# Late weight splits behind the last scatters, later row reads, and a shorter one-hot step in a three-stage kernel

## The chip, the cores and the metric

The program runs on 1 core of one Trainium2 chip. Its time is the device time in microseconds of one execution. The kernel before takes 622.37 us as the median of 3 runs (622.19 to 624.54). The one execution that the profiler took lasted 627.96 us, with a span of 626.2 us from its first to its last instruction.

## The reference

Three layers follow each other. The first is an attention with a state that is updated token by token. The second sends each of the 1536 tokens (2 sequences of 768) to one of 8 experts. The third adds a Fourier transform over tokens and features to each token, normalises, and applies a two-layer perceptron.

```python
def _moe_ref(x, w_gate, w_local, w1, w2):
    ...
            fresh_e = int(np.argmax(logits[b, s]))
            if s == 0 or local_gate[b, s] < 0.5:
                e = fresh_e
            else:
                e = prev_e if prev_e >= 0 else fresh_e
            ...
            h = np.maximum(x[b, s] @ w1[e], 0.0)
            out[b, s] = p[e] * (h @ w2[e])

def _moe2_ref(x, w_ch1, w_ch2):
    X = np.fft.fft(x, axis=1)
    X = np.fft.fft(X, axis=2)
    mixed = np.real(X).astype(np.float32)
    u = x + mixed
    mu = np.mean(u, axis=-1, keepdims=True)
    var = np.mean((u - mu) ** 2, axis=-1, keepdims=True)
    un = (u - mu) / np.sqrt(var + 1e-06)
    ch = np.maximum(un @ w_ch1, 0.0) @ w_ch2
    return (u + ch).astype(np.float32)
```

## The kernel before

Products are made in three passes of split numbers: every fp32 operand becomes a high part (ScalarE, a copy to fp32r) and a low part (VectorE, the original minus the high part), and high*high, low*high and high*low are summed in PSUM.

**Routing** (`route`, L735). From the gate's logits VectorE finds each token's expert (`Ot`, a one-hot row of 8 per token), TensorE counts ranks inside the expert (`rk`, L781 and L783), and VectorE turns the rank into a half (`hi`) and a slot (`rm`). `oh` is the one-hot of the slot; `Wr` carries the token's number in the column of its expert. Thirteen products (`st`, L803) then give a table of token numbers by slot, from which GpSimd gathers rows. `parts` (L811) makes `ph`, number times half, and then `Wr`.

**Experts** (`moe_main`, L940). 32 steps `q`, four for each expert. `whi(q)` (ScalarE, L888) and `wlo(q)` (VectorE, L891) split the step's weights; `wlo(q)` then asks for the weights of step q+6 on the SP queue. `xtr` transposes gathered rows and splits them (L904 to L907), `h` makes the first layer (L916 to L919), `o` the second (L927). At an expert's last step two tiles of results are scaled (`ot`, L932), and `scatter` (L936) writes the rows to their places in `x2d` in DRAM by an indirect DMA that GpSimd issues. `dec` decodes the third layer's weights from a packed form along the way. Behind the last step stand `WARMM` products that fill TensorE's time, `wlo(35)`, and the splits of steps 36 and 37, which are weights of the third layer. The order is that of the code.

**Third layer** (`mixer`, L1375). Each sequence `b` comes back as three blocks of two tiles, `xa` (L1088), in the order 1, 2, 0. Sums and differences of blocks (`sums`, `difs`: tiles `d` and `e`) are split (`zh`, `zl`), multiplied with tables along tokens (`yp`, L1195), evacuated (`Y`) and multiplied along features (`fp`, L1206). Half of the result, `q`, is copied out, `m` combines the halves (L1218, L1219), and `m` is added to `ur`, which holds the sequence's rows in another order: four of six tiles by one SP transfer (L1094), two mirrored ones by indirect DMA (L1098). Then come statistics (`bs`, `ag`, `vs`), the normalised rows `un`, their transpose `up`, its split `uT`, and the perceptron: `mp` (L1330) with `mh` and `ml`, and `mop` (L1356). A further `WARM` products on the first block (L1312) fill TensorE's time before the first `yp`.

The order of this third stage is not that of the code. `Order` (L44) runs generators against assumed costs and emits an engine's next instruction by priority; `eng` (L1103) lets an addition go to VectorE or GpSimd, whichever the plan takes to be done first. So an added wait or another `WARM` moves many instructions.

Of the kernel before, what the change touches and what calls it, by code (L numbers as in the profile page):

```python
# [729 lines left out]
class Rest:  # L730
# [4 lines left out]
    def route(s,keep,pool,ps,lg):  # L735
# [40 lines left out]
        V.tensor_copy(out=e,in_=ei)  # L776
        Ot=s.Ot=pool.tile([128,12,8],F16,name="Ot")
        V.tensor_tensor(out=Ot,in0=it,in1=b3(e),op=ALU.is_equal)

        rk=P("rk",[128,13,8])  # L780
        nc.tensor.matmul(out=rk[:,0:12],lhsT=K["upper"][:,0:128],rhs=Ot,start=True,stop=True,skip_group_check=True)  # L781
        for j in range(12):
            nc.tensor.matmul(out=rk[:,j+1:13],lhsT=ones,rhs=Ot[:,j:j+1].to_broadcast([128,12-j,8]),start=False,stop=True,skip_group_check=True)  # L783
        rank=s.rank=pool.tile([128,12],F32,name="rank")
# [5 lines left out]
        s.Wr=T("W",[128,4,2,12,8],F16); s.ph=T("ph",[128,4,2,12],F16); pp=s.pp=pool.tile([128,4,12],F16,name="pp")  # L790
# [8 lines left out]
        V.tensor_copy(out=pp[:,0],in_=tok)  # L799
        s.parts(0)  # L800
# [139 lines left out]
    def moe_main(s):  # L940
        dec=s.decoding(); s.sc=[]; s.scattered=[]; last=None
        s.chosen()
        s.wlo(0); s.wlo(1)
        for k in range(3): s.xtr(0,k,"h",3)
        s.wlo(2)
        next(dec)
        for q in range(32):
            e,g=divmod(q,4)
            if g==0 and e<7: s.gather(e+1)
            x=s.h(q)  # L950
            if g and e<7: s.xtr(e+1,g-1)
            s.whi(q+4)
            if last: s.o(q-1,last)
            last=x
            s.wlo(q+3)
            if q==1: s.parts(1)
            if q==2: s.parts(2); s.parts(3)
            if q==3: s.slots_p()
            if g==1:
                while s.sc: s.scatter()  # L960
            if q==26: s.tables(0)
            if q==29: s.tables(1)
            if q>2:
                for _ in range(1+(g==0)): next(dec,None)
        for t in range(2):
            s.o(31,last,(t,))
            while s.sc: s.scatter()
        p=s.ps.tile([128,2,256],F32,tag="h",name="wp",bufs=3)
        for _ in range(s.WARMM): s.nc.tensor.matmul(out=p[:,0,0:128],lhsT=s.K["ident"],rhs=s.K["ident"],start=True,stop=True)
        s.wlo(35)  # L970
        for _ in dec: pass
        for q in (36,37):
            s.whi(q); s.wlo(q)

    WARMM=24
# [102 lines left out]
    def load(s,b):  # L1078

        nc,o=s.nc,s.o  # L1080
        yield ("+","xa")
        xa=s.xa[b]={}
        v=s.x2d[768*b:768*b+768].rearrange("(a p) d -> p a d",p=128)
        for n,i in enumerate((1,2,0)):
            yield ("Q",475)
            if n!=1: T=s.rawp.tile([128,1552],F32,tag="raw",name="xa",bufs=6)
            t=T[:,768*(n%2):768*(n%2)+768].rearrange("p (a d) -> p a d",d=384)
            nc.sync.dma_start(out=t,in_=v[:,i:6:3])  # L1088
            xa[i],xa[i+3]=t[:,0],t[:,1]
            o.add(s.arrive(f"xa{b}{i}",1850+1100*n*(1-b)+900))  # L1090
        ur=s.ur[b]=s.fp.tile([128,6,384],F32,tag=f"ur{b}",name="ur",bufs=1)
        w=s.x2d[768*b:768*b+768].rearrange("(p a) d -> p a d",a=6)
        yield ("Q",475)
        nc.sync.dma_start(out=ur[:,0:4],in_=w[:,0:4])  # L1094
        yield f"xa{b}0"
        for k in (4,5):
            yield ("P",1040)
            nc.gpsimd.indirect_dma_start(out=ur[:,k],out_offset=None,in_=s.x2d,in_offset=bass.IndirectOffsetOnAxis(ap=s.K["mirror"][:,2*b+k-4:2*b+k-3],axis=0))  # L1098
        o.add(s.arrive(f"ur{b}",4000))
# [79 lines left out]
    WARM,PHASE=18,0  # L1179
# [303 lines left out]
```

## Time and profile before

| | |
|---|---|
| median of 3 runs | 622.37 us |
| the profiled execution's own time | 627.96 us |
| its span | 626.2 us |
| PE busy | 507.9 us (81%) |
| DVE busy | 421.7 us (67%) |
| ACT busy | 323.7 us (52%) |
| POOL busy | 88.1 us (14%) |
| chain that ended last | PE 38%, issue 13%, POOL 3%, DVE 2% |

The attention takes the span to about 250 us, routing to 267 us, the experts to 410 us and the third layer the rest. The busy shares are means over stages that differ: what counts for an edit is who waits for whom where the edit stands. PE is TensorE, DVE VectorE, ACT ScalarE, POOL GpSimd, SP the engine that issues most transfers.

### The profile page before, as it was taken

The page shows a single profiled execution, that of the slowest core. Times are in us where ns is not written, and L with a number is a line of the kernel's source. Part 1 is how long each engine was busy: PE and PEld are TensorE (multiplying, and loading weights), DVE is VectorE, ACT ScalarE, POOL GpSimd, SP SyncE. Part 2 cuts the span into 40 slices and gives each one's busy share as a digit, 9 for nine tenths or more (in the row PEclk, how much of TensorE's full clock was granted, in tenths as well). Part 3 has the DMA queues.
Part 4 walks back from the last instruction along what each step waited for, and adds up shares of the span by engine and source line. Part 5 has one row for each costly group of instructions (what it writes and reads, how often), then busy time and mean ns, then how long its engine had stood idle before and what let it go on. Part 6 is the DMA issues. An engine that isn't in the chain of part 4 may idle for free.

```text
span 626.2 us, 12592 instructions
## 1 busy us (share of the span) xinstructions
PE 507.9 (81%) x4986; PEld 482.3 (77%) x4986; DVE 421.7 (67%) x950; ACT 323.7 (52%) x745; POOL 88.1 (14%) x89
## 2 busy tenths in 40 slices
PE   0333047894888999599999999978899999999997
PEld 0233037784778898589999999977799998998997
DVE  7968997868997963687788788767886731221122
ACT  3465177877788897346665656543454321111111
POOL 5000000000000000223212232243640000000010
PEclk9955558877989999599999999989699999999999
DMA  6722230341331525699789795235000000010010
GB/s 231 143 59 77 67 62 8 113 93 51 77 70 28 95 49 165 197 312 349 263 286 326 274 304 187 93 133 188 1 1 1 14 13 1 2 50 1 1 50 26
DMA packets 71438, 69.85 MB, mean 112 GB/s; under 512 B 44286, under 2 KB 63523, under 8 KB 71376
## 3 DMA queue, kind: packets, MB, share of 16 engines
q1 hardware_dynamic: 68240, 59.16, 31.8%
q0 software_dynamic: 3136, 9.85, 4.6%
q8 instruction: 40, 0.66, 0.4%
q14 instruction: 22, 0.18, 0.1%
HBM read 53.53 MB, written 7.86 MB: 98 GB/s over the span
## 4 chain that ended last, share of the span: by engine, by line
PE 38%; issue 13%; POOL 3%; DVE 2%; DMA 1%; ACT 1%; POOLq 0%; SPq 0%; ACTq 0%
PE mp L1330 12%; PE mop L1356 12%; PE hp L916 5%; PE op L927 4%; PE fp L1206 2%; PE yp L1195 1%; POOL xg L898 1%; POOL x2d L936 1%; PE up L1288 1%; POOL ur L1098 1%; DMA x2d<-ot,sim 1%; DMA xa<-x2d 0%; POOL e L1109 0%; POOL tab L1074 0%; PE xtp L904 0%
## 5 line engine op out<-in xcount | busy, mean ns | idle before, releaser
L1340 DVE SCALAR_TENSOR_TENSOR ml<-mp,mh 128x256 fp32r<-128x256 f32 (+1 forms) x48 | 26.8, 558 | 98.5 <-ACT mh L1338 98.3
L1330 PE MATMUL mp<-uT,ws 128*128 128x256 f32 (+1 forms) x432 | 85.3, 343 | 0.2 <-DVE ml L1340 0.2
L1338 ACT ACTIVATE mh<-mp 128x256 fp32r<-128x256 f32 (+1 forms) x48 | 23.6, 491 | 115.7 <-PE mp L1330 115.7
L1356 PE MATMUL mop<-ws,mh 128*128 128x384 f32 x288 | 81.6, 338 | 0.0
L1330 PEld LDWEIGHTS mp<-uT,ws 128*128 128x128 f32 x432 | 69.5, 193 | 9.0 <-DVE ml L1340 0.8
L916 PE MATMUL hp<-xT,ws 128*128 128x256 f32 x576 | 74.0, 283 | 1.1 <-DVE xT L907 1.1
L916 PEld LDWEIGHTS hp<-xT,ws 128*128 128x128 f32 x576 | 72.5, 190 | 1.3 <-DVE xT L907 1.3
L927 PE MATMUL op<-ws,hh 128*128 128x384 f32 x256 | 72.1, 343 | 0.0
L309 PEld LDWEIGHTS <-KT 128*128 128x128 f16 x576 | 25.9, 113 | 58.7 <-issue 31.0
L309 PE MATMUL ga<-ST,KT 128*128 128x64 f16 x288 | 16.4, 227 | 57.0 <-DVE ST L305 50.6
L891 DVE TENSOR_TENSOR ws<-raw,ws 128x1536 fp32r<-128x1536 f32 x32 | 56.0, 1751 | 0.0
L1356 PEld LDWEIGHTS mop<-ws,mh 128*128 128x128 f32 x288 | 52.8, 188 | 0.8
L888 ACT ACTIVATE ws<-raw 128x1536 fp32r<-128x1536 f32 x32 | 47.4, 1487 | 2.6 <-DMA raw<-moe_w 2.6
L1356 PE MATMUL mop<-ws,ml 128*128 128x384 f32 x144 | 48.3, 335 | 0.0
L927 PEld LDWEIGHTS op<-ws,hh 128*128 128x128 f32 x256 | 46.8, 188 | 0.0
L927 PE MATMUL op<-ws,hl 128*128 128x384 f32 x128 | 42.9, 335 | 0.0
L919 DVE SCALAR_TENSOR_TENSOR hl<-hp,hh 128x512 fp32r<-128x512 f32 x32 | 22.1, 691 | 27.4 <-ACT hh L918 27.3
L898 POOL DMA_INDIRECT xg<-xd,gm x16 | 21.7, 1356 | 120.4 <-DMA raw<-moe_w 113.7
L918 ACT ACTIVATE hh<-hp 128x512 fp32r<-128x512 f32 x32 | 19.0, 593 | 36.0 <-PE hp L916 36.0
L936 POOL DMA_INDIRECT x2d<-ot,sim x16 | 21.5, 1347 | 101.6 <-ACT ot L932 99.2
L368 DVE TENSOR_TENSOR tmp<-Gu,P 128x31 f32<-128x31 f32 (+15 forms) x93 | 31.5, 339 | 1.9
L370 DVE TENSOR_TENSOR P<-P,tmp 128x31 f32<-128x31 f32 (+15 forms) x93 | 31.4, 337 | 1.7
(268 smaller groups left out, 1224.1 us busy)
## 6 DMA issues: line engine op xcount, KB each, us to landing
raw<-moe_w SPq DMA_DIRECT2D x64, 384.0 KB, 5.5
x<-moe_w_ch SPq DMA_DIRECT2D x24, 384.0 KB, 6.3
qp<-q SPq DMA_DIRECT2D x6, 512.0 KB, 3.9
kp<-k SPq DMA_DIRECT2D x6, 384.0 KB, 4.7
vp<-v SPq DMA_DIRECT2D x6, 384.0 KB, 5.2
xd<-yb SPq DMA_DIRECT2D x48, 48.0 KB, 1.7
xa<-x2d SPq DMA_DIRECT2D x6, 384.0 KB, 4.0
tab<-seq POOLq DMA_DIRECT2D x2, 768.0 KB, 7.2
```

The source lines that it names most:

```text
L309: s.nc.tensor.matmul(out=out,lhsT=st[l],rhs=mv[m],start=(first and i==0),stop=True,skip_group_check=True)
L368: nc.vector.tensor_tensor(out=x,in0=Gu[:,k,k+1:32].unsqueeze(2).to_broadcast([128,m,n]),in1=P[:,k,0:n].unsqueeze(1).to_broadcast([128,m,n] ...
L370: nc.vector.tensor_tensor(out=P[:,k+1:32,0:n],in0=P[:,k+1:32,0:n],in1=x,op=ALU.subtract)
L888: s.nc.scalar.activation(out=s.W[q][:,0].rearrange("p s c -> p (s c)"),in_=s.raw[q],func=AF.Copy)
L891: s.nc.vector.tensor_tensor(out=W[1],in0=s.raw[q],in1=W[0],op=ALU.subtract)
L898: nc.gpsimd.indirect_dma_start(out=s.xg[e][t],out_offset=None,in_=s.xd,in_offset=bass.IndirectOffsetOnAxis(ap=s.gi[:,8*t+e:8*t+e+1],axis=0))
L916: nc.tensor.matmul(out=p[:,i],lhsT=s.W[q][:,a,i,128*k:128*k+128],rhs=xT[b][:,k],start=(n==0),stop=(n==8)); n+=1
L927: nc.tensor.matmul(out=s.po[t],lhsT=hs[a][:,i,128*t:128*t+128],rhs=s.W[q][:,b,i,384:768],start=(g==0 and i==0 and n==0),stop=(g==3 and i== ...
L936: i=s.nc.gpsimd.indirect_dma_start(out=s.x2d,out_offset=bass.IndirectOffsetOnAxis(ap=s.si[:,c:c+1],axis=0),in_=ot,in_offset=None,bounds_ch ...
L1330: nc.tensor.matmul(out=p,lhsT=s.w_ch1(a,k,f),rhs=s.uT[g][b][:,k,0:N],start=(n==0),stop=(n==8)); n+=1
L1340: nc.vector.scalar_tensor_tensor(out=hl,in0=p,scalar=0.0,in1=hh,op0=ALU.max,op1=ALU.subtract)
L1356: nc.tensor.matmul(out=pm[t],lhsT=hs[a][:,128*t:128*t+128],rhs=s.w_ch2(b,f),start=(f==0 and n==0),stop=(f==11 and n==2))
```

## The change

Routing rounds the token numbers earlier and multiplies them with `Ot` beside the rank products; `Wr` is then that product times the half, without `ph`. In the experts, `wlo(1)` stands behind the first `xtr` calls and `wlo(2)` inside step 0. Behind the last step GpSimd writes one column of a small tile `z` after the two scatters, VectorE copies it, and only then come `wlo(35)` and the two last splits. The sequence's own rows `ur` are asked for behind the third block: ScalarE writes one column of `ur` from that block, so that the transfer waits for it. `WARMM` goes from 24 to 38 and `WARM` from 18 to 6.

```diff
+        pp=s.pp=pool.tile([128,4,12],F16,name="pp"); pp0=pp[:,0]
         Ot=s.Ot=pool.tile([128,12,8],F16,name="Ot")
         V.tensor_tensor(out=Ot,in0=it,in1=b3(e),op=ALU.is_equal)
+        V.tensor_copy(out=pp0,in_=tok)
+        Wt=T("Wt",[128,12,8],F16)
...
+        V.tensor_tensor(out=Wt,in0=Ot,in1=b3(pp0),op=ALU.mult)
         rank=s.rank=pool.tile([128,12],F32,name="rank")
...
-        V.tensor_copy(out=pp[:,0],in_=tok)
-        s.parts(0)
+        for h in range(2): V.tensor_tensor(out=s.Wr[:,0,h],in0=Wt,in1=b3(s.hi[:,h]),op=ALU.mult)
...
-        s.wlo(0); s.wlo(1)
+        s.wlo(0)
         for k in range(3): s.xtr(0,k,"h",3)
-        s.wlo(2)
+        s.wlo(1)
         next(dec)
...
+            if q==0: s.wlo(2)
             s.wlo(q+3)
...
+        z=s.wk.tile([128,2],F32,name="z")
+        s.nc.gpsimd.memset(z[:,0:1],0.0)
+        s.nc.vector.tensor_copy(out=z[:,1:2],in_=z[:,0:1])
+        for _ in dec: pass
         s.wlo(35)
-        for _ in dec: pass
         for q in (36,37):
             s.whi(q); s.wlo(q)
 
-    WARMM=24
+    WARMM=38
...
+        yield f"xa{b}0"
+
+        yield ("A",150)
+        nc.scalar.activation(out=ur[:,0,0:1],in_=xa[0][:,0:1],func=AF.Copy)
         yield ("Q",475)
         nc.sync.dma_start(out=ur[:,0:4],in_=w[:,0:4])
-        yield f"xa{b}0"
         for k in (4,5):
...
-    WARM,PHASE=18,0
+    WARM,PHASE=6,0
```

The instructions of GpSimd at the start of the third layer, where it reads the blocks of the first sequence (`e<-xa`), gathers mirrored rows and adds `m` to `ur`. Before:

```order
L936 DMA x2d<-ot,sim 1536x384 x2
L1109 ISA
L1109 TENSOR_TENSOR e_6306<-xa 128x384
L1109 TENSOR_TENSOR e_6307<-xa 128x384
L1098 DMA ur<-x2d,mirror 128x384 x2
L1109 TENSOR_TENSOR e_6306<-e_6306,e_6307 128x384
L1098 DMA ur<-x2d,mirror 128x384 x2
L1109 TENSOR_TENSOR ur<-ur,m 128x384 x2
L1109 TENSOR_TENSOR e_6305<-e_6305,e_6306 128x384
```

And now:

```order
L939 DMA x2d<-ot,sim 1536x384 x2
L976 MEMSET z 128x1
L1120 ISA
L1120 TENSOR_TENSOR e_6324<-xa 128x384
L1120 TENSOR_TENSOR e_6325<-xa 128x384
L1120 TENSOR_TENSOR e_6323<-xa 128x384
L1109 DMA ur<-x2d,mirror 128x384 x2
L1120 TENSOR_TENSOR e_6324<-e_6324,e_6325 128x384
L1109 DMA ur<-x2d,mirror 128x384 x2
L1120 TENSOR_TENSOR ur<-ur,m 128x384 x4
L1120 TENSOR_TENSOR e_6323<-e_6323,e_6324 128x384
```

The third difference of blocks and two more of the additions to `ur` have moved to GpSimd, ahead of its next difference.

VectorE between the evacuations of the transform along tokens and the first statistics (`m` combines halves, `bs` and `ag` are statistics). Before:

```order
L1218 TENSOR_TENSOR m<-fp,q 128x193
L1219 TENSOR_TENSOR m<-fp,q 128x191
L1109 TENSOR_TENSOR ur<-ur,m 128x384
L1231 TENSOR_TENSOR Y<-yp,Y 128x256
L1218 TENSOR_TENSOR m<-fp,q 128x193
L1219 TENSOR_TENSOR m<-fp,q 128x191
L1231 TENSOR_TENSOR Y<-yp,Y 128x256
L1247 BN_STATS bs_6467<-ur 128x6
L1249 BN_AGGR ag<-bs_6467 128x2
L1247 BN_STATS bs_6470<-ur 128x6
```

And now:

```order
L1242 TENSOR_TENSOR Y<-yp,Y 128x256 x5
L1229 TENSOR_TENSOR m<-fp,q 128x193
L1230 TENSOR_TENSOR m<-fp,q 128x191
L1229 TENSOR_TENSOR m<-fp,q 128x193
L1230 TENSOR_TENSOR m<-fp,q 128x191
L1229 TENSOR_TENSOR m<-fp,q 128x193
L1230 TENSOR_TENSOR m<-fp,q 128x191
L1258 BN_STATS bs_6493<-ur 128x6
L1260 BN_AGGR ag<-bs_6493 128x2
L1258 BN_STATS bs_6498<-ur 128x6
```

All evacuations `Y` now stand ahead of the first `m`, three tiles' `m` ahead of the first statistics, and no addition to `ur` is left between them.

ScalarE at the start of the third layer, before:

```order
L1379 ACTIVATE sq<-sq 128x1
L1172 ACTIVATE zh<-d_6302 128x384
L1172 ACTIVATE zh<-d_6303 128x384
L1172 ACTIVATE zh<-e_6329 128x384
L1229 ACTIVATE Y<-yp 128x256 x3
L1172 ACTIVATE zh<-e_6307 128x384
L1211 ACTIVATE q<-fp 128x194
```

And now:

```order
L1390 ACTIVATE sq<-sq 128x1
L1104 ACTIVATE ur<-xa 128x1
L1183 ACTIVATE zh<-d_6320 128x384
L1183 ACTIVATE zh<-d_6321 128x384
L1183 ACTIVATE zh<-e_6344 128x384
L1240 ACTIVATE Y<-yp 128x256
L1183 ACTIVATE zh<-e_6325 128x384
L1104 ACTIVATE ur<-xa 128x1
L1240 ACTIVATE Y<-yp 128x256 x5
L1222 ACTIVATE q<-fp 128x194 x2
```

The two small writes `ur<-xa` are new, the second one (for the second sequence) in front of five evacuations, and the fourth split `zh` has moved ahead of two evacuations.

## Rows read from the trace of the kernel before

**Rows 1.** Windows: stretch, length, busy PE, PEld, DVE, ACT, POOL, clock, DMA share, GB/s.

```profile
416.00:419.50 3.50, 0.00 (x0) 0.01 (x1) 0.10 (x1) 0.00 (x0) 0.00 (x0) 0.83 0.58 187
419.50:426.40 6.90, 6.88 (x36) 6.76 (x36) 4.54 (x7) 1.05 (x2) 4.66 (x4) 0.59 0.73 253
426.40:438.00 11.60, 9.86 (x73) 8.74 (x72) 9.55 (x28) 3.85 (x11) 4.20 (x4) 1.00 0.56 201
438.00:444.70 6.70, 4.06 (x15) 3.11 (x16) 5.49 (x12) 4.03 (x9) 5.62 (x6) 0.56 0.01 2
444.70:449.00 4.30, 4.30 (x20) 4.30 (x21) 3.85 (x7) 0.77 (x2) 2.26 (x3) 0.50 0.00 0
449.00:622.00 173.00, 172.56 (x1046) 161.14 (x1046) 66.81 (x178) 44.30 (x101) 14.83 (x14) 1.00 0.03 12
```

**Rows 2.** Timeline of POOL: start, duration, line, operation, idle before it.

```profile
327.48 1.03 POOL L936 DMA_INDIRECT x2d<-ot,sim  x1 [0.31 <-issue]
...
409.96 2.44 POOL L936 DMA_INDIRECT x2d<-ot,sim  x1 [9.79 <-ACT ot L932]
412.71 2.06 POOL L936 DMA_INDIRECT x2d<-ot,sim  x1 [0.30 <-issue]
419.55 2.54 POOL L1109 TENSOR_TENSOR e<-xa 128x384 f32<-128x384 f32 x2 [4.78 <-DMA xa<-x2d]
...
434.63 1.01 POOL L1109 TENSOR_TENSOR ur<-ur,m 128x384 f32<-128x384 f32 x1 [2.93 <-DVE m L1219]
```

**Rows 3.** Timeline of DVE from the experts into the third layer.

```profile
409.75 1.75 DVE L891 TENSOR_TENSOR ws<-dec,ws 128x1536 fp32r<-128x1536 f32 x1
...
412.12 3.43 DVE L891 TENSOR_TENSOR ws<-dec,ws 128x1536 fp32r<-128x1536 f32 x2 [0.62 <-ACT ws L888]
...
419.40 0.56 DVE L1109 TENSOR_TENSOR d<-xa 128x384 f32<-128x384 f32 x1 [3.85 <-DMA xa<-x2d]
...
421.26 1.24 DVE L1109 TENSOR_TENSOR d<-d,d 128x384 f32<-128x384 f32 x1
423.72 0.57 DVE L1109 TENSOR_TENSOR e<-xa 128x384 f32<-128x384 f32 x1 [1.22 <-DMA xa<-x2d]
```

**Rows 4.** Timeline of SP's queue at the start of the third layer.

```profile
416.29 1.43 SPq L1088 DMA_DIRECT2D xa<-x2d  x3
418.02 0.33 SPq L1094 DMA_DIRECT2D ur<-x2d  x1
```

**Rows 5.** Timeline of ACT from the third layer's start to the first statistics.

```profile
425.26 1.11 ACT L1172 ACTIVATE zh<-d 128x384 fp32r<-128x384 f32 x2 [9.47 <-DVE d L1109]
...
432.11 0.33 ACT L1211 ACTIVATE q<-fp 128x194 f32<-128x194 f32 x1 [0.66 <-PE fp L1206]
...
438.17 0.70 ACT L1272 ACTIVATE un<-ur,vs 128x384 f32<-128x384 f32 x1
```

**Rows 6.** Timeline of PE: fill, first product of the third layer, first of the perceptron.

```profile
409.94 5.52 PE L969 MATMUL wp<-ca 128*128 128x128 f32 x48
...
426.43 0.39 PE L1195 MATMUL yp<-tab,zh 128*128 128x256 f32 x1
...
444.70 2.29 PE L1330 MATMUL mp<-uT,ws 128*128 128x256 f32 x9
```

**Rows 7.** Timeline of DVE in the routing.

```profile
255.60 0.25 DVE L785 TENSOR_TENSOR t<-Ot,rk 128x96 f32<-128x96 f16 x1 [0.87 <-PE rk L783]
...
256.75 0.17 DVE L799 CAST pp<-rc 128x12 f16<-128x12 f32 x1
...
257.15 0.43 DVE L814 TENSOR_TENSOR W<-Ot,ph 128x96 f16<-128x96 f16 x2
```

**Rows 8.** Timeline of all engines at the first expert's first step.

```profile
267.65 0.94 ACT L906 ACTIVATE xT<-xtp 128x256 fp32r<-128x256 f32 x3 [4.39 <-PE xtp L904]
...
268.65 1.08 DVE L907 TENSOR_TENSOR xT<-xtp,xT 128x256 fp32r<-128x256 f32 x3
269.13 4.57 PE L916 MATMUL hp<-xT,ws 128*128 128x256 f32 x36 [1.08 <-DVE xT L907]
```

More of the change, by code (lines that the diff above doesn't have):

```diff
@@ L789, in route @@
         hi=s.hi=T("hi",[128,2,12],F16); lo=T("lo",[128,12],F16)
-        s.Wr=T("W",[128,4,2,12,8],F16); s.ph=T("ph",[128,4,2,12],F16); pp=s.pp=pool.tile([128,4,12],F16,name="pp")
+        s.Wr=T("W",[128,4,2,12,8],F16); s.ph=T("ph",[128,4,2,12],F16)
         oh=s.oh=pool.tile([128,12,128],F16,name="oh")
```

## The prediction

> **What bounds the kernel now.** I read the windows first, then the timelines of the engines at the three places of the change. In the windows the reader is to see that PE is busy for 172.56 of the last 173 us at full clock [rows 1]. So the third layer's end is the start of the perceptron's first product, `mp` at 444.70 [rows 6], plus a fixed amount of PE work, plus what half clock costs on the way. From 426.40 to 444.70 PE has gaps (9.86 busy of 11.60 us, then 4.06 of 6.70 [rows 1]): there VectorE, ScalarE and GpSimd set the pace. The experts' stage before it is a chain of PE work too, so whatever starts it sooner ends it sooner. A part of this change counts only if it moves the first product of the experts (269.13 [rows 8]), the third layer's rows, or the first `mp`.
>
> The sum is made against the profiled execution's own 627.96 us. That is 5.59 above the median of 622.37; I take the differences over unchanged. A measurement of this kernel tells about 0.5%, 3.1 us, from no change.
>
> **Routing.** The cast of the numbers starts at 256.75 and `W` at 257.15 [rows 7]: with cast and `ph` gone from there, 0.40 us of VectorE's serial chain goes. The cast and the product `Wt` are added where VectorE idles 0.87 us for the rank products [rows 7]; at 0.17 and 0.25 us (the rows of the same shapes there) they fit. The gather and everything behind it move by the whole 0.40, since fill products on PE start behind the table and move along. If the cover were gone it would cost 0.42; ends -0.4 and 0, value -0.40.
>
> **First tokens.** ScalarE's three splits of tokens run from 267.65 for 0.94, so the first ends near 268.0, but VectorE's low parts wait until 268.65 because the second weight split stands ahead; the first product follows at 269.13 [rows 8]. With that split behind, low parts start at about 268.1, 0.55 sooner. The 36 products shown are two steps in 4.57 us; the second step, some 2.2 us behind 268.55, needs the second split, which now ends at 268.1+1.08+1.75=270.9: 0.1 is given back. The SP queue sends the weights of step 8 behind six packed loads, and the split of step 2 precedes its use on PE by over a microsecond. If the loads were late the 0.45 would go. Value -0.45, ends -0.55 and 0.
>
> **The last scatters.** The first starts at 409.96 and lasts 2.44, the second 412.71 and 2.06, while one that met no long subtraction lasts 1.03 [rows 2]. VectorE's `wlo(35)` runs from 409.75 to 411.50, the next from 412.12 to about 413.8 [rows 3]; the scatters end 0.9 behind each. So a scatter that meets such a subtraction waits for its end. Without them I get 409.96+1.03+0.30+1.03=412.32 instead of 414.77: 2.45 sooner. The Trainium skill speaks against this part: its page SBUF — State Buffer, section Who interferes with whom, says that a `tensor_tensor` with both inputs in SBUF holds only the read side of the pair that VectorE and GpSimd share, and infers that descriptor generation needs the write side, so it would not be stalled. By that rule the scatters keep their lengths and the 2.45 is zero; the trace disagrees (2.44 against 1.03) and decides. What the rule would make of the time is a rival below.
>
> The wait costs at the other end. Behind the waiting copy VectorE has three subtractions (5.10 us at the 1.67 spacing of the pair in 3.43 [rows 3]), then the third layer's first sum, for which GpSimd and all products wait. GpSimd's write and the semaphore are not shown; between 0.1 and 0.6, I take 0.4. So the subtractions run from 412.7 to 417.85 instead of to 415.55. The first block, asked for at 416.29 and there at 419.40 [rows 3, 4], comes at 413.84+3.11=416.95: now VectorE is late, not the block, and the first sum moves from 419.40 to 417.9, by 1.5 instead of 2.45.
>
> **Rows behind the third block.** VectorE stalls 1.22 us until 423.72 for the third block [rows 3], which shares the transfers with `ur`, asked for at 418.02 [rows 4]. With `ur` behind it, the block should land some 5 us behind the first request (estimate: its place in the three 384 KB transfers at the rate of [rows 1], 253 GB/s and more), near 419: the stall goes. What is late next is the pair of engines. GpSimd's two differences take 2.54 and VectorE's third sum 1.24 instead of 0.56 beside them [rows 2, 3]: sums of SBUF tiles alternate, some 1.27 a pair. Now GpSimd has three of them, held until 417.85. Three pairs end near 421.7, VectorE's two free sums (0.5 each) near 422.7, and `zh` starts there instead of 425.26 [rows 5]: 2.5 sooner. With it the first `yp`, 426.43 [rows 6], moves to 423.9.
>
> `ur` itself is needed only at `m`, over 8 us later, and lands in time. The write for the second sequence stands on ScalarE ahead of five evacuations and waits for that sequence's third block. With its request at about 423.4 and 4 to 6.5 us to land (the third block of the first sequence took up to 423.72-416.29=7.4 from the first request), it costs 0 to 1.9; I take 0.3.
>
> **The new order.** From `q` to the first `un` the trace takes 6.06 us [rows 5]. There one addition ran on VectorE and one on GpSimd (1.01 [rows 2]), and statistics of the first tile lay beside the latter. Now both run on GpSimd in series, through one buffer `m`; a third tile's `m` stands ahead of the statistics and a fourth inside them (about 0.63 each); both tiles' statistics come behind. Extra: 0.65 for the second addition, 1.26 for the two pairs, 0.9 for uncovered statistics, less 0.8 for two `Y` that stood there: 2.0. Ahead of `q`, 18 products of the next pair now stand before or between the transforms (about 2.2 us), so `q` comes at about 432.4 although the stage starts 2.5 sooner. Behind `un`, 1.3 comes back since the second `un` no longer waits behind `uT`. First `mp`: 444.70+0.3+2.0-1.3=445.7, 1.0 later than before. The other end is that all steps keep their distances: 2.5 sooner. I cannot weigh the overlaps from the rows; I take -0.7, near the middle, and keep both ends.
>
> **Fill.** 38 products take 8.74 us at the rate of 5.52 for 24 [rows 6], to 418.7; 6 more to 420.1. They stand where PE has nothing, at no cost. Then PE idles about 3.8 us. Before, an idle of 4.05 let the granted clock fall (0.83 in 416.00 to 419.50), and the 36 fill matmuls ran mostly at the lower level (0.59), so that the real products from 426.40 had 1.00 [rows 1]. Now the first `yp` may meet half clock. I take nothing for it in the sum: evacuation waits on ScalarE's splits anyway. If it lasts, see below.
>
> Sum: -0.40-0.45-0.70=-1.55, so 626.4 for an execution like the profiled one and 620.8 for the median. Within 0.5%.
>
> **The rivals.** *The front is kept.* The added serial steps hide, first `mp` comes 2.5 sooner and the first perceptron products do not meet half clock as they did (0.50 for 4.30 busy us from 444.70 [rows 1], worth up to 2.15). For it: the planner places steps by when it thinks inputs arrive, and the added work lies on an engine with idle time. Against: one buffer `m` forces the series. -0.40-0.55-2.5=-3.45 up to -5.6; time 617.8.
>
> *Half clock through the sparse stretch.* The clock falls in the idle behind the shorter fill and does not return before the dense products. For it: with 4.06 busy of 6.70 us it was 0.56 [rows 1]; against: `yp` is dense for 3 us right at the start, and 5.5 us of dense fill brought it back before. The 9.86 busy us from 426.40 would double; some 4.2 of them (the second pair's products and the transforms up to `q`) are serial. It decides once more than about half of that is hit. First `mp` 1.0+4.2 later, less 0.85: +4.3, 626.7. This is the side of slower.
>
> *The scatters keep their lengths*, GpSimd being bound by something else. Then the subtractions start at 415.1 and end at 420.3, the first sum 0.9 later than before, `zh` as before, the order's 3.5 us uncovered: +2.6, 625.0. Against it stand the 1.03 and 2.44.
>
> **Chances.** Forecast 0.46 (own range 619.3 to 623), front kept 0.34, half clock 0.13, scatters unchanged 0.04, other 0.03. Faster by over 0.5%: the second case and a tail of the first, 0.36. Slower by over 0.5%: most of the third and some of the fourth, 0.14. Within: 0.50. The range from 615.8 to 625.4 leaves out about 1 in 10 on either side.
>
> **What would show it.** Right: scatters of about 1.0 us without a subtraction beside them; VectorE's first sum directly behind the last subtraction, with no wait for a block; no wait of ScalarE over 1 us at the second `ur<-xa`; four additions to `ur` in a row on GpSimd; over 7.5 us from `q` to `un`; `mp` at 442 to 445. Wrong: scatters as long as before; `mp` before 441; a clock below 1.00 for most of the stretch between first `yp` and `mp`.

## Result: slower by 1.4%, and where the profile after shows it

The changed kernel takes 631.98 us (median of 4 runs, 629.7 to 633.69) against 622.37; the ratio is 1.0144 [1.0103, 1.0185], outside the predicted range. The profiled execution took 633.69 us with a span of 631.9, 5.7 longer than the span before.

Executions differ in the attention, which the change doesn't touch: over the 17 traces of this study the first product behind it, routing's `fp` (L772), starts between 249.76 and 255.34 us. So I count from that start (253.53 before, 253.19 after) and call it the gate product. "Experts end" is the start of the fill `wp` behind the experts. The other columns are the first instruction of that name, each counted from the column before; "end" is the end of the span:

| us | experts end | first `yp` | `q` | `un` | first `mp` | end | sum |
|---|---|---|---|---|---|---|---|
| before | 156.41 | 16.49 | 5.68 | 6.06 | 6.53 | 181.50 | 372.67 |
| after | 154.49 | 14.24 | 11.63 | 10.54 | 6.40 | 181.41 | 378.71 |
| difference | -1.92 | -2.25 | +5.95 | +4.48 | -0.13 | -0.09 | +6.04 |

The intended savings come: 4.17 us are gained up to the first `yp`. Then 10.43 are lost in two steps, ahead of `q` and between `q` and `un`. The timelines of GpSimd and VectorE after (start, duration, engine, line, operation, in brackets the idle time before it and what ended it), against [rows 2, 3]:

```profile
407.71 1.03 POOL L939 DMA_INDIRECT x2d<-ot,sim  x1 [9.71 <-ACT ot L935]
409.04 1.01 POOL L939 DMA_INDIRECT x2d<-ot,sim  x1 [0.30 <-issue]
416.04 3.80 POOL L1120 TENSOR_TENSOR e<-xa 128x384 f32<-128x384 f32 x3 [5.88 <-DMA xa<-x2d]
...
434.62 0.99 POOL L1120 TENSOR_TENSOR ur<-ur,m 128x384 f32<-128x384 f32 x1 [7.61 <-DVE m L1230]
436.34 0.99 POOL L1120 TENSOR_TENSOR ur<-ur,m 128x384 f32<-128x384 f32 x1 [0.73 <-DVE m L1230]
438.07 0.99 POOL L1120 TENSOR_TENSOR ur<-ur,m 128x384 f32<-128x384 f32 x1 [0.73 <-DVE m L1230]
440.14 0.99 POOL L1120 TENSOR_TENSOR ur<-ur,m 128x384 f32<-128x384 f32 x1 [1.08 <-DVE vs L1268]
441.09 0.99 POOL L1120 TENSOR_TENSOR e<-e,e 128x384 f32<-128x384 f32 x1
442.04 1.95 POOL L1120 TENSOR_TENSOR d<-xa 128x384 f32<-128x384 f32 x2
```

```profile
410.20 0.15 DVE L977 COPY z<-z 128x1 f32<-128x1 f32 x1 [2.63 <-POOL z L976]
410.27 5.08 DVE L894 TENSOR_TENSOR ws<-dec,ws 128x1536 fp32r<-128x1536 f32 x3
...
415.90 0.56 DVE L1120 TENSOR_TENSOR d<-xa 128x384 f32<-128x384 f32 x1 [0.54 <-DMA xa<-x2d]
...
439.98 0.15 DVE L1268 RECIPROCAL vs<-vs 128x2 f32<-128x2 f32 x1
440.17 0.98 DVE L1270 TENSOR_TENSOR vs<-vs 128x2 f32<-128x2 f32 x1
441.19 0.92 DVE L1272 TENSOR_TENSOR vs<-vs 128x2 f32<-128x2 f32 x1
442.14 0.93 DVE L1274 TENSOR_SCALAR vs<-vs 128x2 f32<-128x2 f32 x1
443.10 0.17 DVE L1276 RECIPROCAL vs<-vs 128x2 f32<-128x2 f32 x1
443.30 0.71 DVE L1278 SCALAR_TENSOR_TENSOR vs<-ag,vs 128x2 f32<-128x2 f32 x1
```

The scatters take 1.03 and 1.01 instead of 2.44 and 2.06. From 434.62 on, four `ur` additions stand on GpSimd, 1.7 to 2.1 apart, since each waits for its `m`. Behind the fourth, three sums of blocks follow at once (`e<-e,e` and two `d<-xa`). The statistics on VectorE suffer beside these four last instructions of GpSimd: operations on two numbers per partition take 0.71 to 0.98 us there, while the reciprocal among them, at 443.10, takes 0.17. Before, GpSimd was idle at this place, and such an operation took 0.16:

```profile
437.13 0.16 DVE L1259 TENSOR_TENSOR vs<-vs 128x2 f32<-128x2 f32 x1
```

ScalarE and TensorE after, against [rows 5, 6, 8]:

```profile
418.22 0.20 ACT L1104 ACTIVATE ur<-xa 128x1 f32<-128x1 f32 x1 [2.62 <-DMA xa<-x2d]
420.76 1.11 ACT L1183 ACTIVATE zh<-d 128x384 fp32r<-128x384 f32 x2 [2.33 <-DVE d L1120]
...
428.17 0.20 ACT L1104 ACTIVATE ur<-xa 128x1 f32<-128x1 f32 x1 [1.91 <-DMA xa<-x2d]
...
433.55 0.34 ACT L1222 ACTIVATE q<-fp 128x194 f32<-128x194 f32 x1 [1.60 <-PE fp L1217]
...
444.09 1.30 ACT L1283 ACTIVATE un<-ur,vs 128x384 f32<-128x384 f32 x2 [4.31 <-DVE vs L1278]
```

```profile
267.93 2.33 PE L919 MATMUL hp<-xT,ws 128*128 128x256 f32 x18 [0.50 <-DVE xT L910]
...
421.92 0.58 PE L1206 MATMUL yp<-tab,zh 128*128 128x256 f32 x1 [4.25 <-ACT zh L1183]
...
429.97 0.81 PE L1217 MATMUL fp<-tab,Y 128*128 128x194 f32 x6
430.62 0.30 PE L1206 MATMUL yp<-tab,zh 128*128 128x256 f32 x1
...
431.36 3.49 PE L1217 MATMUL fp<-tab,Y 128*128 128x194 f32 x30
444.85 0.90 PE L1299 MATMUL up<-ca,un 128*128 128x128 f32 x3 [10.00 <-ACT un L1283]
...
450.49 1.80 PE L1341 MATMUL mp<-uT,ws 128*128 128x256 f32 x8
```

Before, the first 18 `yp` [rows 6] are followed at once by 18 `fp`:

```profile
429.81 2.26 PE L1206 MATMUL fp<-tab,Y 128*128 128x194 f32 x18 [0.39 <-DVE Y L1231]
```

Now 30 `yp` products come first, then 6 `fp`, 6 `yp`, 30 `fp`, and `q` can start only inside the last group. Behind it TensorE has nothing for 10.00 us. The windows after, by stage (columns as in [rows 1]: start:end, length, busy time of PE, PEld, DVE, ACT and POOL, granted clock, DMA share, GB/s):

```profile
417.70:421.90 4.20, 0.00 (x0) 0.00 (x0) 3.55 (x5) 1.25 (x3) 3.74 (x4) 0.93 0.59 180
421.90:428.20 6.30, 6.25 (x24) 5.42 (x24) 3.77 (x7) 1.46 (x4) 3.60 (x4) 0.51 0.89 303
428.20:434.90 6.70, 5.79 (x49) 5.52 (x48) 2.56 (x7) 2.10 (x7) 0.28 (x1) 1.00 0.40 133
434.90:444.80 9.90, 0.00 (x0) 0.00 (x0) 7.74 (x20) 1.25 (x4) 6.54 (x7) 0.67 0.00 0
444.80:450.50 5.70, 4.20 (x19) 3.80 (x20) 5.40 (x13) 3.64 (x9) 1.00 (x1) 0.50 0.01 3
```

The first `yp` ran at the lower clock level (0.51) behind an idle 4.2 us, and so did the work behind the idle 9.9 (0.50).

### The profile page after: what moved, and what is told of

It is laid out like the page before. It is cut to its first block, busy times and chain, and to the rows that moved or that the text cites. A ratio compares the mean times of both kernels' runs of the same rounds, so it can differ in the third digit from the quotient of the medians.

```text
span 631.9 us, 12599 instructions
## 1 busy us (share of the span) xinstructions
PE 506.0 (80%) x4990; PEld 482.2 (76%) x4990; DVE 424.6 (67%) x951; ACT 324.7 (51%) x747; POOL 85.6 (14%) x90
## 4 chain that ended last, share of the span: by engine, by line
PE 37%; issue 12%; POOL 4%; DVE 3%; DMA 1%; POOLq 0%; ACT 0%; DVEq 0%; SPq 0%
PE mop L1367 12%; PE mp L1341 12%; PE hp L919 5%; PE op L930 4%; PE yp L1206 2%; PE fp L1217 2%; POOL xg L901 1%; PE up L1299 1%; POOL ur L1109 1%; POOL e L1120 1%; DMA x2d<-ot,sim 1%; POOL x2d L939 1%; DMA xa<-x2d 1%; PE xtp L907 0%; POOL tab L1082 0%
## 5 line engine op out<-in xcount | busy, mean ns | idle before, releaser
L939 POOL DMA_INDIRECT x2d<-ot,sim x16 | 19.1, 1192 | 99.0 <-ACT ot L935 96.6
```

What stands on the lines that cost most here:

```text
L939: i=s.nc.gpsimd.indirect_dma_start(out=s.x2d,out_offset=bass.IndirectOffsetOnAxis(ap=s.si[:,c:c+1],axis=0),in_=ot,in_offset=None,bounds_ch ...
```

## Experiments

Theory ORDER: the new order of the third layer loses more than the scatters and the third block bring. Its rivals are CLOCK (the shorter fill, with half clock behind it), BLOCKED ACT (ScalarE held by the second `ur<-xa`), SUM ROWS LATE (the `ur` rows arrive too late), SCATTERS (the later splits hold ScalarE or VectorE) and LEAD LOST ANYWAY (what arrives earlier is lost again at the third layer's start). The kernel before had medians of 625.0 to 626.6 beside these runs, so times are compared as ratios to it, and traces by the table's columns.

**Parts (a) and (b) alone.** The change has five parts: (a) is routing, (b) the second and third weight split moved later, (c) the wait behind the scatters and `WARMM`, (d) the row requests, (e) `WARM`. Against the changed kernel, in extracts:

```diff
-        z=s.wk.tile([128,2],F32,name="z")
-        s.nc.gpsimd.memset(z[:,0:1],0.0)
-        s.nc.vector.tensor_copy(out=z[:,1:2],in_=z[:,0:1])
+        s.wlo(35)
         for _ in dec: pass
-        s.wlo(35)
...
-    WARMM=38
+    WARMM=24
...
-        yield f"xa{b}0"
-
-        yield ("A",150)
-        nc.scalar.activation(out=ur[:,0,0:1],in_=xa[0][:,0:1],func=AF.Copy)
         yield ("Q",475)
         nc.sync.dma_start(out=ur[:,0:4],in_=w[:,0:4])
+        yield f"xa{b}0"
...
-    WARM,PHASE=6,0
+    WARM,PHASE=18,0
```

> Parts (a) and (b) alone: the token-number product beside the ranks, and the second and third weight splits later. The end of the experts is issued as before, the fill is 18 and the third layer's order is that of before, row for row. Theory ORDER (the two front parts and the two intended mechanisms all pay, and the new order of the third layer's instructions loses more than they bring): the first hidden-layer products start near 268.0 us of the span (before 269.13), the experts end near 408.0 (before 409.94), and all of it is kept, since nothing behind it moves: 620.2 us, between 619.7 and 621.0. Rival LEAD LOST ANYWAY (whatever arrives earlier at the third layer is lost there, because its start waits for something with a time of its own): 622.4, between 621.8 and 622.9.

Measured 0.994 [0.9908, 0.9971], more than the 0.9965 expected. The experts end at 154.57; `yp`, `q` and `un` follow 16.50, 5.67 and 6.07 behind each other. So the 1.84 us of lead is kept, against LEAD LOST ANYWAY. The sum is 368.46, 4.2 below before. The other 2.4 us stand behind `un`, and go with the clock: it was 0.94 in the 3 us from the first `mp`, where before had 0.50 for 4.30 us [rows 1], with the same instructions in the same order. The ratio, 3.7 us, is nearer to the 4.2 than to the 1.84, so ordinary executions of before seem to lose part of this too. Over the sixteen traces of the other kernels the ratio taken as time lies 1.4 us above the difference of the sums on average; by that estimate the 6.04 us between the profiles of before and after stand for some 7.4 of the 9.0 us of the ratio (622.37 x 0.0144), whose interval goes from 6.4 to 11.5.

**With (c).** The same kernel, with the wait `z` and `WARMM=38` kept.

> Parts (a), (b) and (c): the last three weight splits behind the last scatters too, 38 products of fill there; rows and fill of the third layer, and its order, as before. Theory ORDER: the scatters fall to 1.03 and 1.01 us, the three blocks are asked for about 3.6 us sooner than 416.29, but the request for the sum rows stands behind them in the queue as before, so the third block comes with its old delay: first product of the third layer near 423 (before 426.43), and the end 2 to 4 us before that of the kernel before: 619.0, between 617.8 and 620.6. Rival SCATTERS (the later splits are what costs, since they hold ACT or DVE at the third layer's start): 622.5 or more.

Measured 0.996 [0.9936, 0.9985], against SCATTERS, which wanted no gain. The scatters took 1.03 and 1.01. The first `yp` comes 15.70 behind the experts' end (16.50 without (c)), but `q` 6.56 behind it (5.67): the clock was 0.72 in the 6 us from the first `yp`. The 2.5 us of the ratio lie within the 2 to 4 expected against before, but they are those of (a) and (b): the sum is 368.6 with (c) and 368.46 without it. In this trace the shorter scatters bring 0.8 and lose it to the clock.

**With the first sequence's write, in the order of before.** Against the kernel with (a) to (c):

```diff
+        if b==0: nc.scalar.activation(out=ur[:,0,0:1],in_=xa[0][:,0:1],func=AF.Copy)
         yield ("Q",475)
         nc.sync.dma_start(out=ur[:,0:4],in_=w[:,0:4])
         yield f"xa{b}0"
```

> Parts (a), (b), (c), and of (d) the first sequence's one-column write only, put ahead of the request for the sum rows without a turn in the planner, so that the third layer's order stays that of before; fill of 18. Theory ORDER: third block about 3 us sooner than in the kernel with (a) to (c), the sum rows about 5 us later but still ahead of the first ur addition (which waits for its FFT products): first product near 421.9 as in the changed kernel, the sixth mp chain still 10 us earlier than the changed kernel's 450.49: 617.5, between 616.0 and 619.5. Rival SUM ROWS LATE (the rows for the sum, not the order, hold the additions of the changed kernel): about 624 or more, with additions waiting for a DMA. Rival CLOCK (the clock falls in the shorter wait too): some 2 us more than ORDER, 619.5.

Measured 0.9923 [0.9885, 0.9961], as expected. The first `yp` comes 13.73 behind the experts' end: asking for the `ur` rows behind the third block brings another 1.97 here. `q` follows 5.67 behind, `un` 6.07, the first `mp` 5.59; the sum is 366.46. Counted from the gate product, ScalarE's `q` and first `un` of this kernel come 6.4 and 10.9 us ahead of those after:

```profile
423.98 0.33 ACT L1220 ACTIVATE q<-fp 128x194 f32<-128x194 f32 x1 [0.66 <-PE fp L1215]
...
430.05 0.70 ACT L1281 ACTIVATE un<-ur,vs 128x384 f32<-128x384 f32 x1
```

Against SUM ROWS LATE: no addition to `ur` on GpSimd waits for a transfer, neither here nor after. The same kernel a second time:

> The kernel with parts (a) to (c), the first sequence's one-column write and the order of before, once more, beside the two others of this call. Theory ORDER: ratio 0.9923 as measured, between 0.989 and 0.9955. If the first figure was a lucky one: 0.996 or above.

Measured 0.9925 [0.9889, 0.996]. In this trace the first `yp` comes 14.30 behind the experts' end, so the rows' request is worth 1.4 to 2.0; the sum is 367.17.

**The new order alone, on the kernel before.** The planner is told of the wait, the write and 6 products; no write is emitted, and 18 products are:

```diff
+        yield f"xa{b}0"
+        yield ("A",150)
         yield ("Q",475)
         nc.sync.dma_start(out=ur[:,0:4],in_=w[:,0:4])
-        yield f"xa{b}0"
...
-    WARM,PHASE=18,0
+    WARM,PHASE=6,0
...
-            s.nc.tensor.matmul(out=p[:,0:128],lhsT=x,rhs=x,start=True,stop=True)
+            for _ in range(3): s.nc.tensor.matmul(out=p[:,0:128],lhsT=x,rhs=x,start=True,stop=True)
```

> The kernel before with the changed kernel's order of the third layer and nothing else: the planner is told of the wait for the third block, of the one-column write (which isn't emitted) and of 6 products of fill, while 18 are emitted. Blocks, scatters and routing as before. Theory ORDER: the four ur additions stand on POOL in series, the statistics between them are held, and the first mp comes 6 to 9 us later than 444.70: 631, between 628 and 635. Rival CLOCK (the shorter fill and the half clock behind it make the loss): near 622.5, since the fill is full. Rival BLOCKED ACT (ACT's wait for the second sequence's third block makes the loss): 622.5 to 624, since the write that waits is left out.

Measured 1.0195 [1.016, 1.0231]; `q` comes 10.00 behind the first `yp` and `un` 10.55 behind `q`, and the sum is 382.01. With the scatters and the fill as before and no write on ScalarE, the order alone costs 9.3 us by the traces (12 by the ratio). CLOCK and BLOCKED ACT as whole causes fall: the clock was 1.00 from the first `yp` to `q`. GpSimd and ScalarE of this kernel:

```profile
436.35 1.00 POOL L1110 TENSOR_TENSOR ur<-ur,m 128x384 f32<-128x384 f32 x1 [5.93 <-DVE m L1220]
438.08 0.99 POOL L1110 TENSOR_TENSOR ur<-ur,m 128x384 f32<-128x384 f32 x1 [0.73 <-DVE m L1220]
439.81 0.99 POOL L1110 TENSOR_TENSOR ur<-ur,m 128x384 f32<-128x384 f32 x1 [0.73 <-DVE m L1220]
441.88 0.99 POOL L1110 TENSOR_TENSOR ur<-ur,m 128x384 f32<-128x384 f32 x1 [1.08 <-DVE vs L1258]
```

```profile
435.28 0.33 ACT L1212 ACTIVATE q<-fp 128x194 f32<-128x194 f32 x1 [1.60 <-PE fp L1207]
...
445.83 1.30 ACT L1273 ACTIVATE un<-ur,vs 128x384 f32<-128x384 f32 x2 [4.31 <-DVE vs L1268]
```

**The changed kernel with the order put right.** In `along`:

```diff
+        if (b,k2)==(0,1): yield "f02"
         yield ("+","Y")
...
+        if (b,k2)==(0,2): yield ("!","f02")
         yield ("-","Y")
```

> The changed kernel with all its parts, fill of 6 and both one-column writes, and one constraint more: the second pair's chain of the first sequence (a01) waits, in the planner, until the first pair's chain (a02) has issued its fp products. That one constraint gives the order of before back almost row for row. Theory ORDER: from the first yp to the first q 5.7 to 6.8 us (11.63 in the changed kernel, 5.68 before), from q to un 6.1 to 7.0 (10.54 and 6.06), and the time is below that of the kernel before: ratio 0.993, between 0.989 and 0.998. Rival FILL AND WRITES (the shorter fill, with half clock at the first yp, or ACT's wait for the second sequence's third block, make a good part of the loss whatever the order): ratio 1.000 or above.

Measured 1.0003 [0.9972, 1.0034]: the order alone gives 1.4% back, but the kernel is no faster than before, which is the rival's figure (FILL AND WRITES). `q` comes 8.47 behind the first `yp`, `un` 6.33, first `mp` 5.58; the sum is 370.34. So the order is worth 378.71-370.34=8.4 us, and fill and writes cost 370.34-366.46=3.9 against the kernel with the first write and 18 of fill (3.2 against its second trace). ScalarE here waits for the second sequence, just ahead of the `Y` that the first `fp` need:

```profile
424.50 0.20 ACT L1104 ACTIVATE ur<-xa 128x1 f32<-128x1 f32 x1 [1.64 <-DMA xa<-x2d]
424.61 0.64 ACT L1242 ACTIVATE Y<-yp 128x256 fp32r<-128x256 f32 x2
427.00 0.33 ACT L1224 ACTIVATE q<-fp 128x194 f32<-128x194 f32 x1 [1.75 <-PE fp L1218]
```

**The order of before, 6 of fill.** Against the kernel with the first sequence's write:

```diff
-            s.nc.tensor.matmul(out=p[:,0:128],lhsT=x,rhs=x,...)
+            if _<6: s.nc.tensor.matmul(out=p[:,0:128],lhsT=x,rhs=x,...)
```

> The kernel with parts (a) to (c), the first sequence's one-column write and the order of before, with 6 products of fill issued where the planner is told of 18. It tells what the clock at the first yp is worth in a good order. Theory ORDER: the 18 products of the first pair run at half clock (4.2 us, not 3.0), of which the evacuations on ACT hide part: first mp 0.4 to 1.2 us later from the gate's product than with 18, ratio 0.994, between 0.991 and 0.9975 (0.9923 with 18). Rival CLOCK (half clock at the start costs several us): 1.000 or above.

Measured 0.9967 [0.9937, 0.9998], within what ORDER allowed; but `q` comes 7.59 behind the first `yp` (5.67 with 18), and the first `mp` 1.5 to 2.4 later from the gate product than in the two traces with 18, where 0.4 to 1.2 was allowed. From the first `yp` to `q`, first this kernel, then the one with 18:

```profile
424.10:431.70 7.60, 7.56 (x38) 7.27 (x39) 4.61 (x9) 2.20 (x5) 2.99 (x3) 0.57 1.02 382
```

```profile
418.30:424.00 5.70, 5.08 (x38) 4.55 (x38) 4.43 (x9) 2.11 (x6) 3.19 (x3) 1.00 0.99 356
```

The same 38 recorded products span 1.9 us more at a mean clock of 0.57. Up to `q` nothing hides it. The remaining 0.88 to the 8.47 above most likely goes with the second write, the main difference that is left.

**The changed kernel, fill issued threefold.** `for _ in range(3):` ahead of the fill's product.

> The changed kernel with 18 products of fill in the third layer, where the planner is told of 6 as in the changed kernel: every engine keeps the changed kernel's order. Theory ORDER: the chain from the first product to the first mp is bound by the engines behind TensorE (POOL's additions and DVE's small operations), so the clock at the first products matters little: 631, between 629.5 and 632.5. Rival CLOCK: the idle 4.25 us ahead of the first product is filled to about 2, the 18 products behind it run at full clock (3.0 us, not 4.2) and the time falls to 627 or below.

Measured 1.0137 [1.0098, 1.0176], sum 381.77: no gain, yet not a clean test of the fill. The clock was 1.00 at the first `yp`, but ScalarE's second write waits 2.60 (1.91 after) and ends 0.7 later from the first `yp`, though the second sequence's blocks are asked for at the same distance from it; why they come later isn't shown. TensorE then stands idle, and the half clock falls on the products behind; `q` is 14.45 behind the first `yp`:

```profile
431.70:435.70 4.00, 3.99 (x18) 4.00 (x19) 1.04 (x3) 0.42 (x2) 0.00 (x0) 0.50 0.63 201
```

**The changed kernel without the second write.** `if b==0:` stands ahead of ScalarE's write.

> The changed kernel without the second sequence's one-column write, so that ACT does not wait at 428.17 for that sequence's third block; the order of all else stays. Theory ORDER: this wait is 1.9 us on ACT, in a stretch where ACT is late for the conversion of the second group of products; the fp chain and what follows come up to 1.5 us sooner: 631, between 629.5 and 632.3. Rival BLOCKED ACT: the wait starts the whole loss, and without it the time falls to 626 or below.

Measured 1.0101 [1.0065, 1.0138], somewhat more back than expected; `q` 10.40 (11.63), `un` 10.55, sum 376.79, 1.9 below after. BLOCKED ACT is worth 1.2 us at `q`, not the loss.

**The changed kernel, first sequence's `ur` additions on VectorE**, in place, the plan untouched: `if x[0]=="q": e=s.nc.vector` in `tt`. (The second sequence's stood on VectorE already.)

> The changed kernel with the first sequence's six ur additions emitted on VectorE where the planner put them on POOL; all else in the changed kernel's order. Theory ORDER by the SHARED STALL (small DVE operations of the statistics take 0.7 to 0.98 us beside POOL's additions, and the additions stand in series): the additions take some 0.5 us each, the small operations 0.15 again, the scaled copy un ends its wait 4 to 6 us sooner than 444.09: 626, between 624 and 628.5. Rival CLOCK or BLOCKED ACT: the additions lie beside other waits, and the time moves by less than 1 us from the changed kernel's 632.

Measured 1.005 [1.002, 1.0081]; `q` comes 11.00 behind the first `yp`, `un` 7.92 behind `q` (10.54 after), and the sum is 375.37. The small operations are short again; where GpSimd works beside one, it is long again:

```profile
440.00 0.16 DVE L1271 TENSOR_TENSOR vs<-vs 128x2 f32<-128x2 f32 x1
440.19 0.16 DVE L1273 TENSOR_TENSOR vs<-vs 128x2 f32<-128x2 f32 x1
440.39 0.17 DVE L1275 TENSOR_SCALAR vs<-vs 128x2 f32<-128x2 f32 x1
...
442.67 0.97 DVE L1265 TENSOR_SCALAR vs<-ag 128x2 f32<-128x2 f32 x1
```

```profile
442.62 0.99 POOL L1121 TENSOR_TENSOR d<-xa 128x384 f32<-128x384 f32 x1 [12.55 <-DVE d L1121]
```

The four operations from 440.17 after took 3.54, here 0.65: 2.9. From `q` to the reciprocal ahead of them it is 6.43 after, 6.73 here and 4.82 before. So moving the additions shortened nothing but the small operations, and of the 4.48 between `q` and `un` the stall is 2.9 and the longer series of `m`, additions and statistics 1.6. The instructions of GpSimd that stalled them after were one `ur` addition and the three sums of blocks that had queued behind it.

**The changed kernel, fill of 18 told to the planner** (`WARM` 18).

> The changed kernel with a fill of 18, told to the planner too, which makes a third order of the third layer's instructions. Theory ORDER: the time is that order's own, not that of the fill: anything between 618 and 632 with the clock at the first products full; the interval from first q to first un tells it (6 us in before, 10.5 in the changed kernel). Rival CLOCK: 627 or below whatever the order.

Measured 0.9957 [0.9924, 0.999]. It is a third order, with `fp` behind the first 18 `yp` as before: `q` 5.67, `un` 6.44, first `mp` 7.33, sum 368.03. The expectation allowed 618 to 632 us, so its time tells nothing for or against ORDER. Four of the five parts with the planner's own order beat the kernel before; one number, `WARM`, which sets both fill and plan, decided the sign.

**Fill in the idle time ahead of the first transposes.** The changed kernel gets 78, then 36 products there. The kernel with the order of before gets 8 ahead of the first and 10 ahead of the second transposes, then 4 and 5. In `untr`, where N is that number:

```diff
+        if N:
+            pw=s.ps.tile([128,512],F32,tag="o",name="wq",bufs=4)
+            for _ in range(N): nc.tensor.matmul(out=pw[:,0:128],lhsT=s.K["ident"],rhs=s.K["ident"],start=True,stop=True)
         for j in range(3): nc.tensor.transpose(p[:,j],un[:,128*j:128*j+128],s.K["ident"])
```

> The changed kernel, its order kept, with 78 products of fill in TensorE's 10 us of idle time ahead of the first transposes (at 0.115 us each they end about 1 us before these). It tells which part of the changed kernel's loss is clock behind that idle time. Theory ORDER: the clock is 1.00 in the second pair's work and in the first mp chains, and about 2.5 us come back of the loss: ratio 1.010, between 1.007 and 1.0125. Rival CLOCK (half clock makes most of the loss of 9.6 us): 1.003 or below.

Measured 1.0191 [1.0142, 1.024]. A product is two instructions in the trace; 78 products took 17.6 us (156 records), not 9, and the transposes came 8.00 behind `un` (0.76). From there to the first `mp` it is 4.39 instead of 5.64, at a clock of 1.00: full clock is worth 1.25 here.

> The changed kernel, its order kept, with 36 products of fill (0.23 us each, 8.1 in all) in TensorE's 10 us of idle time ahead of the first transposes; the 78 of the run before took 16 us and pushed the transposes back by 7.2, of which 1.2 came back before the first mp. Theory ORDER: the first transposes start as in the changed kernel, from there to the first mp 4.4 us (5.64), another 0.5 to 1 us behind it, so 1.2 to 2.2 us of the loss are clock behind this idle time: ratio 1.0115, between 1.008 and 1.015. Rival CLOCK (most of the loss): 1.005 or below.

Measured 1.0122 [1.0082, 1.0163], sum 378.71 as without. The clock was 1.00 up to 444 and 0.50 from there; the fill had ended 2 us ahead of the transposes at 443.36:

```profile
434.00:444.00 10.00, 7.95 (x70) 7.52 (x68) 8.44 (x21) 1.90 (x5) 5.95 (x7) 1.00 0.00 0
444.00:447.00 3.00, 1.28 (x6) 1.29 (x7) 2.97 (x8) 1.78 (x5) 0.99 (x1) 0.50 0.00 0
```

So the gain expected of full clock was not tested, though the ratio lies within the range.

> The kernel with parts (a) to (c), the first sequence's one-column write and the order of before, with 8 products of fill ahead of the first transposes and 10 ahead of the second, where TensorE idles 1.08 and 1.27 us. If it is that sparse stretch that lets the granted clock fall to 0.50 from about 432 to 439, the clock stays at 1.00, the second pair's products and the first mp chains are faster by about 3 us of their 6.5: first mp 1.0 to 1.3 us sooner and the rest another 1.5: ratio 0.988, between 0.985 and 0.991. If the clock falls all the same: ratio 0.9923, as without.

Measured 0.9932 [0.9902, 0.9963]: there was too much fill here as well. The first `mp` comes 6.56 behind `un` (5.59 without), which is given back later (the end is 179.70 behind the first `mp`, 180.86 without).

> The kernel with parts (a) to (c), the first sequence's one-column write and the order of before, with 4 products of fill ahead of the first transposes and 5 ahead of the second. A product of fill took 0.23 us (two instructions of 0.113), so these take 0.9 and 1.1 us, inside idle times of 1.08 and 1.27; the 8 and 10 of the run before took twice that and pushed the transposes back. Theory ORDER with the clock as the second term: un to first transpose 0.75, from there to the first mp 3.9 to 4.3 us (4.84 without), end 1.0 to 2.0 us sooner than without: ratio 0.990, between 0.987 and 0.993. If the fill is too thin to keep the clock: as without, 0.9923.

Measured 0.9911 [0.987, 0.9952], sum 365.81 against 367.17 and 366.46 without. The clock stayed at 1.00 from the first `yp` to the first `mp` and behind it, but `un` to first `mp` is 5.59 as without, not the shorter one expected: the first `mp` waits for an evacuation of VectorE.

```profile
438.03 1.32 PE L1343 MATMUL mp<-uT,ws 128*128 128x256 f32 x9 [0.87 <-DVE Y L1240]
```

The interval holds the ratio without the fill; as a gain over that it isn't shown. This and the kernel without the fill are the fastest that ran, both faster than before and after.

## Why the prediction was wrong

The failed step is **The new order**, its term "I take -0.7, near the middle" between 2.5 sooner and 1.0 later. Against before, each profile counted from its gate product, the third layer's first `mp` came 8.05 us later than the experts' end allowed (experts end -1.92, first `mp` +6.13), 10.30 later than the first `yp` did. So the far end of 1.0 later was too low as well; with the order alone put right, 8.4 us came back.

- *Routing, first tokens*: -0.85 forecast, -0.86 measured at the first `hp`, about half of it at the table of token numbers. The experts' products took another 1.06 less, which wasn't forecast.
- *The last scatters*: their lengths were right, 1.03 and 1.01. The wait on GpSimd's write cost little (copy at 410.20, 0.15 behind the second scatter's end), and the first sum came 0.54 behind the last subtraction, when a block arrived; I had VectorE late. From the experts' end the sum came 1.24 sooner (1.5 forecast), and that is luck: the blocks were asked for only 1.38 sooner, not 2.45, since 2.60 passed from the second scatter's end to the request, where it was 1.52 before.

```profile
412.65 1.43 SPq L1096 DMA_DIRECT2D xa<-x2d  x3
```

- *Rows behind the third block*: right in kind. The first `yp` came 2.25 sooner from the experts' end, 2.5 forecast, by other steps than those of the sum.
- *Ahead of `q`*: 18 products of the second pair, 2.2 us, were counted, 5.95 measured. With full clock and no second write it is 4.3 (10.00 against 5.68, in the kernel with the new order alone); the second write adds 1.2 (0.3 was taken), and the 0.4 that is left may be clock, though the shorter fill cost 1.9 in the order of before: the parts don't simply add. I had weighed the products alone; `q` waited as well for the second pair's splits and evacuations, which stand on ScalarE and VectorE ahead of the `Y` of the first. (The 432.4 for `q` is also a slip: 2.5 sooner and 2.2 and 0.3 later give 432.1.)
- *From `q` to `un`*: 2.0 forecast, 4.48 measured. Missing was that the "uncovered statistics" would not run at their own length beside GpSimd: 2.9 us, shown by moving the additions; the 1.6 that is left is about the 2.0. The Trainium skill has the rule (SBUF — State Buffer, section Who interferes with whom): a VectorE instruction with two SBUF inputs contends with a GpSimd instruction that reads SBUF, one with a single input outside the two-port modes doesn't, and the later one blocks. The trace agrees: 0.98 us for `tensor_tensor` against 0.16 without GpSimd beside it, 0.17 for the reciprocal, and 0.93 for `tensor_scalar`, which the section names among the operations that can enter a two-port mode. I had used that page for the scatters and not looked for its victims in the new order.
- *Behind `un`*: 1.3 back was forecast, 0.13 came. Before, this stretch held more half clock than in other traces of the same order (6.53 against 5.59), so measured against those the new order took 0.8 longer here.
- *Fill*: "I take nothing for it ... evacuation waits on ScalarE's splits anyway" was wrong: 1.9 us up to `q` in the order of before. The half-clock rival had the sign; the larger part of its price was order.

Of the signs named beforehand, the scatters, the four additions in a row and the time from `q` to `un` (10.54) came as the forecast had them. The first sum's wait, ScalarE's wait at the second write (1.91) and `mp` at 450.49 did not, and the clock was below 1.00 for most of the stretch from the first `yp` to `mp`, a sign named for "wrong".

*The front is kept* is near what came where the order was kept: 0.9923 x 622.37 = 617.6 us, for 617.8 in that rival. That kernel has 18 of fill and one write, though; with the changed kernel's own fill and writes the kept order gave 1.0003.

## What to carry to other kernels

Where a planner sets the order, an edit to its costs or waits is an edit to the whole stage: run the data change in the old order and the new order with the old data, before any term is summed. Read the new order for what stands ahead of the first consumer on every engine, not only on the engine that issues it, and look which short serial operations come to lie beside GpSimd's elementwise work. Fill that looks idle may be what keeps the next products at full clock: here 12 products fewer cost the products behind them 1.9 us.

## What the runs showed of the hardware

- Operations of 2 elements per partition on VectorE took 0.92 to 0.98 us (`tensor_tensor`, `tensor_scalar`) and 0.71 (`scalar_tensor_tensor`) beside GpSimd's `tensor_tensor` of 384 elements per partition, and 0.16 to 0.17 without; the one `reciprocal` beside it stayed at 0.17. The ones of 0.92 to 0.98 are about as long as one instruction of GpSimd (0.99).
- A scatter that met a subtraction of VectorE of 128x1536, both inputs in SBUF, took 2.44 and 2.06 us and ended 0.9 behind a subtraction's end; without one it took 1.03 and 1.01.
- The experts' products from the first `hp` to the fill took 140.81 us in the two kernels without (a) and (b), and 139.75 to 139.82 in the others, about 33 ns less for each of 32 steps, spread over all of them, at a clock of 1.00 and with TensorE busy throughout in both. No wait in the trace accounts for it; it stays open.
